# Retention and a quick-GELU layer: transposing q and k by 32x32 squares on VectorE, products of y in order of shape, row decay applied to y

## The chip, the cores and the metric

One core of a Trainium2 chip. The metric is the time of one execution in device microseconds, lower is better. The profile's span is 1.7 us shorter than the time of the execution it was taken from.

## The reference, cut to what matters

```python
batch, n_heads, seq, head_dim = (4, 8, 768, 64)          # q, k, v, float32
n_tokens, d_model, d_ff = (3072, 512, 2048)              # w_in 512x2048, w_out 2048x512, float64

for t in range(S):                                       # retention, per head
    state = gamma * state + outer(k[:, :, t], v[:, :, t])
    y[:, :, t] = scale * (q[:, :, t] @ state)
x = y.transpose(0, 2, 1, 3).reshape(B * S, H * D)        # 3072 x 512
h = x @ w_in
out = (h * (1.0 / (1.0 + np.exp(-1.702 * h)))) @ w_out
```

## The kernel before

Retention runs in 24 chunks of 128 tokens, six for each of the four sequences. A chunk has three stages: `turn` puts channels on partitions, `attend` makes the scores, `finish` makes y and the next state. Four chunks are a block of 512 tokens; a block's layer is 32 units of four 128x512 products, and the chunks of one block run between the units of the block before. The weights come as the bits of float64, in 32 pieces of 512 KB (`raw`), and `narrow` turns one piece into float32 with six VectorE instructions, two of ScalarE and one of GpSimd.

```python
    def load(j):
        b, c = divmod(j, NC)
        for name, src in (("q", q), ("k", k), ("v", v)):
            t = loads.tile([P, H, D], F32, name=name + "_in")
            sp.dma_start(t, src[b, :, c * P:(c + 1) * P, :].rearrange("h p d -> p h d"))
            QKV[name, j] = t
    # ... cut
    def turn(j):
        qn, kn = QKV.pop(("q", j)), QKV.pop(("k", j))
        for x, store in ((qn, QT), (kn, KT)):
            p = ps.tile([P, HP, P], F32, name="pt", tag="att")
            for hp in range(HP):
                pe.transpose(p[:, hp, :], x[:, 2 * hp:2 * hp + 2, :].rearrange("p i d -> p (i d)"), ident)
            t = work.tile([P, HP, P], F32, name="qT" if store is QT else "kT")
            if store is QT:
                dve.tensor_mul(t, p, rowd)
            else:
                act.activation(t, p, AF.Copy)
            store[j] = t
    # ... cut (kd = k times its decay, on GpSimd)
    def finish(j):
        # ... cut
        for hp in range(HP):
            if c:
                pe.matmul(y[:, hp, :], old[:, hp, :], qt[:, hp, :], start=True, stop=False)
            for i in range(2):
                pe.matmul(y[i * D:(i + 1) * D, hp, :], vn[:, 2 * hp + i, :], a[:, i, hp, :],
                          start=not c, stop=True)
        # ... cut
        act.activation(XT[m][:, :, n * P:(n + 1) * P], y, AF.Copy)
    # ... cut
    # chunks of block m between the units of block m - 1 (take runs units, and narrows a weight beside each)
                if j + AHEAD < NCH:
                    load(j + AHEAD)
                turn(j)
                take(per // 4)
                attend(j)
                take(per // 4)
                finish(j)
                take(per - 2 * (per // 4))
                if m == 0:
                    for _ in range(N1 // CB):
                        narrow(pieces.pop(0))      # and fetches the piece three further on, from SyncE's queue
```

Of the kernel before, what the change touches and what calls it, by code (L numbers as in the profile page):

```python
# [8 lines left out]

F32 = mybir.dt.float32  # L10
U32 = mybir.dt.uint32
AF = mybir.ActivationFunctionType
ALU = mybir.AluOpType
P = 128
# [3 lines left out]
    return struct.unpack("<f", struct.pack("<I", bits))[0]  # L18


# Bounds of a float64's high word without its sign, as the float32 of the same bits (which has
# the same order): the exponent below float32's normal numbers, which turns to 0, and 2^128,
# which turns to infinity.
F64_LEAST = _f32((1023 - 127) << 20)
F64_MOST = _f32((1023 + 128) << 20)

# [2 lines left out]
def kernel(  # L29
# [8 lines left out]
    col_decay: bass.AP,  # L38
    out: bass.AP,
):  # L40
    """Retention in chunks of P tokens, its output kept transposed on chip as the x of
    (x @ w_in) * sigmoid(1.702 x @ w_in) @ w_out.

    Within a chunk, y[t] = sum over s <= t of g^(t-s) scale (q[t].k[s]) v[s], plus
    g^(t+1) scale q[t] @ state; then state = g^P state + sum over s of g^(P-1-s) k[s] v[s]^T.
    The weights come as the bits of float64 and are rounded to float32 on chip.
    row_decay[h, t] is scale g^(t+1). col_decay has, by columns: g^-(s+1) [H],
    g^(P-1-s) [H], and g^P [H/2] with its upper half of partitions for a pair's second head.
    """
    nc = tc.nc  # L50
    pe, act, dve, pool, sp = nc.tensor, nc.scalar, nc.vector, nc.gpsimd, nc.sync

    B, H, S, D = q.shape
    NT, DM = out.shape
    DFF = moe_w_in.shape[1]
    HP = H // 2            # pairs of heads: one pair fills the partitions
    NC = S // P            # chunks of a batch
    NCH = B * NC           # chunks
    CB = 4                 # chunks in a block of tokens of the second part
    BT = CB * P  # L60
    NB = NCH // CB
    NFF = DFF // P
# [3 lines left out]
    const = ctx.enter_context(tc.tile_pool(name="const", bufs=1))  # L66
    loads = ctx.enter_context(tc.tile_pool(name="loads", bufs=3))
# [2 lines left out]
    ps_a = ctx.enter_context(tc.tile_pool(name="ps_a", bufs=1, space=bass.MemoryType.PSUM))  # L70
    ps = ctx.enter_context(tc.tile_pool(name="ps", bufs=3, space=bass.MemoryType.PSUM))

# [1 line left out]
    QKV = {}  # L74

    def load(j):
        b, c = divmod(j, NC)
        for name, src in (("q", q), ("k", k), ("v", v)):
            t = loads.tile([P, H, D], F32, name=name + "_in")
            sp.dma_start(t, src[b, :, c * P:(c + 1) * P, :].rearrange("h p d -> p h d"))  # L80
            QKV[name, j] = t

    AHEAD = 2
    rowd = const.tile([P, HP, P], F32, name="rowd")
    cold = const.tile([P, 2 * H + HP], F32, name="cold")
    act.dma_start(cold, col_decay)
# [4 lines left out]
                    ap=[[0, D], [2 * P, HP], [1, P]]),  # L91
        )

    # Weights by pieces of DM columns: w_in's by quarters of its columns, then w_out's by rows.
    W1 = const.tile([P, HP, DFF], F32, name="W1")
    W2 = const.tile([P, NFF, DM], F32, name="W2")
    w1v = moe_w_in.bitcast(U32).rearrange("(c p) (f two) -> p c f two", p=P, two=2)
# [9 lines left out]
            sp.dma_start(RAW[i], PIECES[i][1])  # L107

    def narrow(i):
        """float64 to float32: the high word's 20 bits of fraction with the exponent rebiased, plus  # L110
        the low word at its place, added and so rounded in float32, then the sign."""
        fetch(i + WAHEAD)
        w, x = PIECES[i][0], RAW.pop(i)
        lo, hi = x[:, :, 0], x[:, :, 1]
        m = work.tile([P, DM], F32, name="m")
        e = work.tile([P, DM], F32, name="e")
        r = work.tile([P, DM], F32, name="r")
        mu = m.bitcast(U32)
        dve.tensor_scalar(mu, hi, 0x7FFFFFFF, None, op0=ALU.bitwise_and)  # L119
        dve.tensor_scalar(m, m, F64_MOST, F64_LEAST, op0=ALU.min, op1=ALU.max)  # L120
        # The exponent's bits 10 and 6..0 are those of float32, and 128 more puts bit 10 at bit 7.
        act.activation(m, m, AF.Copy, scale=2.0 ** 16)
        dve.tensor_scalar(mu, mu, 4, 1, op0=ALU.logical_shift_left, op1=ALU.logical_shift_right)  # L123
        dve.tensor_scalar(e.bitcast(U32), mu, 0x7F800000, None, op0=ALU.bitwise_and)  # L124
        act.activation(r, lo, AF.Copy, scale=2.0 ** -52)  # L125
        pool.tensor_mul(r, r, e)  # L126
        dve.tensor_add(m, m, r)  # L127
        dve.scalar_tensor_tensor(w.bitcast(U32), hi, 0x80000000, mu, op0=ALU.bitwise_and, op1=ALU.bitwise_or)  # L128
# [4 lines left out]
        if i < AHEAD - 1:  # L133
            load(i + 1)

# [1 line left out]
    ident = const.tile([P, P], F32, name="ident")  # L137
    make_identity(nc, ident)
    # mask[s, i, hp, t] = g^-(s+1) where s <= t, else 0, for head 2 hp + i
    mask = const.tile([P, 2, HP, P], F32, name="mask")  # L140
    for i in range(2):
        for hp in range(HP):
            h = 2 * hp + i
# [1 line left out]
    m3 = mask.rearrange("s i h t -> s (i h) t")  # L145
    pool.affine_select(out=m3, in_=m3, compare_op=ALU.is_ge, fill=0.0, base=0,
                       pattern=[[0, H], [1, P]], channel_multiplier=-1)
    # two states in turn, block diagonal over a pair's heads
    state = [const.tile([P, HP, P], F32, name=f"state{i}") for i in range(2)]
    for t in state:  # L150
        dve.memset(t, 0.0)

# [1 line left out]
    QT, KT, KD, AT, XT = {}, {}, {}, {}, {}  # L154

    def turn(j):
        """q and k with channels on partitions, q decayed from the chunk's start; k decayed to its end."""
        qn, kn = QKV.pop(("q", j)), QKV.pop(("k", j))
        for x, store in ((qn, QT), (kn, KT)):
            p = ps.tile([P, HP, P], F32, name="pt", tag="att")  # L160
            for hp in range(HP):
                pe.transpose(p[:, hp, :], x[:, 2 * hp:2 * hp + 2, :].rearrange("p i d -> p (i d)"), ident)  # L162
            t = work.tile([P, HP, P], F32, name="qT" if store is QT else "kT")
            if store is QT:
                dve.tensor_mul(t, p, rowd)  # L165
            else:
                act.activation(t, p, AF.Copy)  # L167
            store[j] = t
        if j % NC < NC - 1:
            KD[j] = work.tile([P, H, D], F32, name="kd")  # L170
            pool.tensor_mul(KD[j], kn, cold[:, H:2 * H, None].to_broadcast([P, H, D]))  # L171

    def attend(j):
        p = ps_a.tile([P, 2, HP, P], F32, name="pa")
# [9 lines left out]
    def finish(j):  # L184
        c = j % NC
        old, new = state[c % 2], state[(c + 1) % 2]
        vn, a, qt = QKV.pop(("v", j)), AT.pop(j), QT.pop(j)
        y = ps.tile([P, HP, P], F32, name="py", tag="att")
        for hp in range(HP):
            if c:  # L190
                pe.matmul(y[:, hp, :], old[:, hp, :], qt[:, hp, :], start=True, stop=False)  # L191
            for i in range(2):
                pe.matmul(y[i * D:(i + 1) * D, hp, :], vn[:, 2 * hp + i, :], a[:, i, hp, :],  # L193
                          start=not c, stop=True)
        m, n = divmod(j, CB)
        if n == 0:
            XT[m] = work.tile([P, HP, BT], F32, name="xT")
        act.activation(XT[m][:, :, n * P:(n + 1) * P], y, AF.Copy)  # L198
        if c == NC - 1:
            return  # L200
        kd = KD.pop(j)
        u = ps.tile([P, HP, P], F32, name="pu", tag="att")
        for hp in range(HP):
            h = slice(2 * hp, 2 * hp + 2)
            pe.matmul(u[:, hp, :], kd[:, h, :].rearrange("p i d -> p (i d)"),  # L205
                      vn[:, h, :].rearrange("p i d -> p (i d)"), start=True, stop=True)
        for i in range(2):
            r = slice(i * D, (i + 1) * D)
            if c == 0:
                dve.tensor_copy(new[r, :, r], u[r, :, r])  # L210
            else:
                pool.tensor_mul(new[r, :, r], old[r, :, r],  # L212
                                cold[r, 2 * H:, None].to_broadcast([D, HP, D]))
                dve.tensor_add(new[r, :, r], new[r, :, r], u[r, :, r])  # L214

# [1 line left out]
    GT, PO = {}, {}  # L217

    def up(m, f):
# [22 lines left out]
        return [lambda f=f: up(m, f) for f in range(NFF)] + [  # L242
            lambda n=n, i=i: down(m, n, i) for n in range(CB) for i in range(4)]

# [1 line left out]
    pieces = list(range(len(PIECES)))  # L246
    for m in range(NB + 1):
        todo = units(m - 1) if m else []
# [8 lines left out]
        if m < NB:  # L257
            for n in range(CB):
                j = m * CB + n
# [17 lines left out]


def _decays(n_heads, head_dim):
    """Powers of the heads' decays, which depend on the shapes alone."""  # L280
    import numpy as _np

    gamma = 1.0 - 2.0 ** (-5.0 - _np.arange(n_heads))
    t = _np.arange(P)
    row = gamma[:, None] ** (t + 1) / _np.sqrt(head_dim)
    whole = _np.repeat(gamma.reshape(-1, 2).T ** P, P // 2, axis=0)
    col = _np.concatenate(
        [gamma[None, :] ** -(t[:, None] + 1.0), gamma[None, :] ** (P - 1 - t[:, None]), whole], axis=1)
    return {"row_decay": row.astype(_np.float32), "col_decay": col.astype(_np.float32)}
# [28 lines left out]
```

## Time and profile before

| of the kernel before | us |
|---|---|
| time, median of 2 executions | 856.79 (856.55 to 857.04) |
| first 128x512 product (block 0 starts) | 65.15 |
| first product of block 1 | 209.82 |
| from there to the end | 645.3 |
| TensorE busy | 821.2 of the span's 855.1 |

The table cuts the span at two landmarks: the **head** (loads, weights and chunks 0 to 3, then block 0 with chunks 4 to 7) and the **steady part** after it, where TensorE doesn't stop.

What feeds the head is SyncE's queue, which issues all loads of q, k, v and the weights. In time order, some of its lines (start, length, engine, line, the transfer, how many in a row):

```profile
0.81 0.43 SPq L80 DMA_DIRECT2D q_in<-in_q_dram  x1
...
1.92 0.86 SPq L80 DMA_DIRECT2D v_in<-in_v_dram  x1
2.82 0.97 SPq L107 DMA_DIRECT2D raw<-in_moe_w_in_dram  x1
...
31.79 3.77 SPq L80 DMA_DIRECT2D v_in<-in_v_dram  x1
...
130.72 11.32 SPq L107 DMA_DIRECT2D raw<-in_moe_w_out_dram  x4
```

A chunk costs this queue three issues. Load 3 is the one that block 0 still needs, and what the head waits for is the narrowing.

### The profile page before, as it was taken

The numbers are of one execution on the slowest core, as the hardware profiler recorded it, in microseconds if no ns is written. First come the engines' busy times: TensorE is split into PE (matmuls) and PEld (weight loads), VectorE is DVE, ScalarE is ACT, GpSimd is POOL, SyncE is SP. The second block draws the span as 40 slices with busy tenths as digits, with TensorE's granted clock in tenths as the row PEclk, the third lists the DMA queues.
The fourth block names the chain that finished last, engine by engine and source line by source line (L and its number), as shares of the span: only waits on it lengthen the run. The fifth ranks groups of instructions, "written<-read, shape, count | busy, mean of one in ns | idle before, by whom it ended". The sixth has DMA issues, their size and how long they took to land.

```text
span 855.1 us, 7038 instructions
## 1 busy us (share of the span) xinstructions
PE 821.2 (96%) x2816; PEld 408.3 (48%) x2816; DVE 239.1 (28%) x434; ACT 126.4 (15%) x210; POOL 84.6 (10%) x91
## 2 busy tenths in 40 slices
PE   4679979999999999999999999999999999999998
PEld 3545434445545544544545454445445445444443
DVE  4877888311222110222111222111122111012000
ACT  2234444000111000111000111100011100011000
POOL 3433333201101000101011000011010000000000
PEclk9759989999999999999999999999999999999999
DMA  9476454012010210110110110111100000000000
GB/s 224 133 183 162 149 164 144 25 38 61 13 25 13 50 38 25 50 25 13 38 49 25 37 36 14 25 46 41 38 13 0 1 12 25 12 1 0 13 13 25
DMA packets 83663, 42.66 MB, mean 50 GB/s; under 512 B 75952, under 2 KB 76464, under 8 KB 83632
## 3 DMA queue, kind: packets, MB, share of 16 engines
q1 hardware_dynamic: 79488, 35.66, 16.5%
q10 hardware_dynamic: 4144, 6.57, 2.1%
q8 instruction: 22, 0.36, 0.2%
q14 instruction: 9, 0.07, 0.0%
HBM read 35.92 MB, written 6.29 MB: 49 GB/s over the span
## 4 chain that ended last, share of the span: by engine, by line
PE 87%; DVE 7%; POOL 3%; issue 2%; DMA 1%; ACT 0%; SPq 0%; POOLq 0%; ACTq 0%; DVEq 0%
PE po L234 39%; PE ph L222 34%; PE py L193 4%; PE py L191 3%; PE pa L178 3%; POOL r L126 2%; PE pu L205 2%; PE pt L162 2%; DVE m L127 2%; DVE e L124 1%; DVE m L123 1%; DMA raw<-in_moe_w_in_dram 1%; DVE W L128 1%; DVE m L119 1%; DVE m L120 1%
## 5 line engine op out<-in xcount | busy, mean ns | idle before, releaser
L222 PE MATMUL ph<-xT,W 128*128 128x512 f32 x768 | 340.8, 601 | 0.0
L234 PE MATMUL po<-W,gT 128*128 128x512 f32 x768 | 336.0, 594 | 0.0
L222 PEld LDWEIGHTS ph<-xT,W 128*128 128x128 f32 x768 | 145.5, 193 | 174.0 <-issue 170.9
L234 PEld LDWEIGHTS po<-W,gT 128*128 128x128 f32 x768 | 143.5, 190 | 170.9 <-issue 169.7
L226 DVE TENSOR_TENSOR gT<-ph,sg 128x512 f32<-128x512 f32 x96 | 66.2, 690 | 209.5 <-ACT sg L224 209.5
L224 ACT ACTIVATE sg<-ph 128x512 f32<-128x512 f32 x96 | 57.2, 595 | 261.8 <-PE ph L222 261.7
L237 DVE COPY o<-po 128x512 f32<-128x512 f32 x24 | 16.6, 692 | 239.2 <-PE po L234 239.2
L171 POOL TENSOR_TENSOR kd<-k_in,cold 128x512 f32<-128x512 f32 x20 | 21.1, 1054 | 451.8 <-PE pu L205 258.1
L193 PE MATMUL py<-at,v_in 128*64 128x128 f32 x384 | 46.8, 321 | 14.4 <-DVE at L181 14.4
L181 DVE TENSOR_TENSOR at<-pa,mask 128x512 f32<-128x512 f32 x48 | 31.2, 683 | 67.1 <-PE pa L178 67.1
L126 POOL TENSOR_TENSOR r<-r,e 128x512 f32<-128x512 f32 x32 | 42.3, 1322 | 72.6 <-DVE e L124 72.4
L198 ACT ACTIVATE xT<-py 128x512 f32<-128x512 f32 x24 | 14.3, 596 | 189.3 <-PE py L193 189.3
L191 PE MATMUL py<-qT,state 128*128 128x128 f32 x160 | 41.3, 344 | 0.0
L178 PE MATMUL pa<-qT,kT 64*128 64x128 f32 x384 | 30.4, 302 | 8.6 <-DVE qT L165 7.8
L191 PEld LDWEIGHTS py<-qT,state 128*128 128x128 f32 x160 | 28.0, 209 | 20.5 <-issue 19.7
L178 PEld LDWEIGHTS pa<-qT,kT 64*128 64x128 f32 x384 | 25.6, 203 | 24.9 <-issue 14.6
L193 PEld LDWEIGHTS py<-at,v_in 128*64 128x64 f32 x384 | 22.5, 148 | 29.6 <-DVE at L181 17.4
L167 ACT ACTIVATE kT<-pt 128x512 f32<-128x512 f32 x24 | 14.3, 596 | 142.4 <-PE pt L162 142.4
L127 DVE TENSOR_TENSOR m<-m,r 128x512 f32<-128x512 f32 x32 | 26.2, 819 | 19.4 <-POOL r L126 19.4
L125 ACT ACTIVATE r<-raw 128x512 f32<-128x512 uint32 x32 | 21.8, 681 | 53.9 <-DVE m L127 43.8
L205 PE MATMUL pu<-v_in,kd 128*128 128x128 f32 x160 | 25.8, 307 | 0.0
L212 POOL TENSOR_TENSOR state<-state,cold 64x256 f32<-64x256 f32 x32 | 20.1, 629 | 49.9 <-DVE state L214 31.8
(25 smaller groups left out, 218.0 us busy)
## 6 DMA issues: line engine op xcount, KB each, us to landing
raw<-in_moe_w_in_dram SPq DMA_DIRECT2D x16, 512.0 KB, 4.5
raw<-in_moe_w_out_dram SPq DMA_DIRECT2D x16, 512.0 KB, 3.3
q_in<-in_q_dram SPq DMA_DIRECT2D x24, 256.0 KB, 4.0
k_in<-in_k_dram SPq DMA_DIRECT2D x24, 256.0 KB, 4.4
v_in<-in_v_dram SPq DMA_DIRECT2D x24, 256.0 KB, 3.3
out_dram<-o ACTq DMA_DIRECT2D x24, 256.0 KB, 2.0
rowd<-in_row_decay_dram ACTq DMA_DIRECT2D x2, 128.0 KB, 5.5
cold<-in_col_decay_dram ACTq DMA_DIRECT2D x1, 10.0 KB, 2.8
```

Of the source, the lines that this page charges most:

```text
L125: act.activation(r, lo, AF.Copy, scale=2.0 ** -52)
L126: pool.tensor_mul(r, r, e)
L127: dve.tensor_add(m, m, r)
L178: pe.matmul(p[:, i, hp, :], KT[j][r, hp, :], QT[j][r, hp, :], start=True, stop=True)
L181: dve.tensor_mul(AT[j][:, i], p[:, i], mask[:, i])
L191: pe.matmul(y[:, hp, :], old[:, hp, :], qt[:, hp, :], start=True, stop=False)
L193: pe.matmul(y[i * D:(i + 1) * D, hp, :], vn[:, 2 * hp + i, :], a[:, i, hp, :], start=not c, stop=True)
L205: pe.matmul(u[:, hp, :], kd[:, h, :].rearrange("p i d -> p (i d)"), vn[:, h, :].rearrange("p i d -> p (i d)"), start=True, stop=True)
L222: pe.matmul(p, W1[:, c, f * P:(f + 1) * P], XT[m][:, c, :], start=(c == 0), stop=(c == HP - 1))
L224: act.activation(s, p, AF.Sigmoid, scale=1.702)
L226: dve.tensor_mul(g, p, s)
L234: pe.matmul(p, GT[m, f][:, n * P:(n + 1) * P], W2[:, f, :], start=(f == 0), stop=(f == NFF - 1))
```

## The change

The intent: take the eight transposes of a chunk off TensorE, which sets the time, and spare it changes of shape. The VectorE instruction used, `dve.transpose`, turns each 32x32 block where it stands; so the DMA puts each 32x32 square of q and k at the place of its mirror image, and one such instruction then finishes the transpose of 128x512. As q is no longer decayed on its way out of PSUM, the decay moves to y. k is also loaded in rows (`kn`), for the state.

```diff
     def load(j):
-        for name, src in (("q", q), ("k", k), ("v", v)):
+        for name, src in (("q", q), ("k", k)):
+            t = loads.tile([P, HP, Q4, C4], F32, name=name + "_sq")        # Q4 = 4, C4 = 32
+            for i in range(2):
+                for d in range(D // C4):
+                    r0 = i * D + d * C4
+                    for hp in range(HP):
+                        sp.dma_start(
+                            t[r0:r0 + C4, hp],
+                            src[b, 2 * hp + i, c * P:(c + 1) * P, d * C4:(d + 1) * C4].rearrange(
+                                "(s p) d -> p s d", p=C4))
+            QKV[name, j] = t
+        for name, src in (("kn", k), ("v", v)):
+            if name == "kn" and c == NC - 1:
+                continue
             t = loads.tile([P, H, D], F32, name=name + "_in")
             sp.dma_start(t, src[b, :, c * P:(c + 1) * P, :].rearrange("h p d -> p h d"))
 ... (turn: the PE transposes, the decay of q and the copy of k go)
-            p = ps.tile([P, HP, P], F32, name="pt", tag="att")
-            for hp in range(HP):
-                pe.transpose(p[:, hp, :], x[:, 2 * hp:2 * hp + 2, :].rearrange("p i d -> p (i d)"), ident)
+            dve.transpose(t.rearrange("p h t -> p (h t)"), QKV.pop((name, j)).rearrange("p h s d -> p (h s d)"))
 ... (finish)
+        if c:
+            for hp in range(HP):
+                pe.matmul(y[:, hp, :], old[:, hp, :], qt[:, hp, :], start=(hp == 0), stop=False,
+                          skip_group_check=True)
         for hp in range(HP):
-            if c:
-                pe.matmul(y[:, hp, :], old[:, hp, :], qt[:, hp, :], start=True, stop=False)
             for i in range(2):
                 pe.matmul(y[i * D:(i + 1) * D, hp, :], vn[:, 2 * hp + i, :], a[:, i, hp, :],
-                          start=not c, stop=True)
+                          start=(not c and hp == 0), stop=(hp == HP - 1), skip_group_check=True)
-        act.activation(XT[m][:, :, n * P:(n + 1) * P], y, AF.Copy)
+        dve.tensor_mul(XT[m][:, :, n * P:(n + 1) * P], y, rowd)
```

More of the change, by code (lines that the diff above doesn't have):

```diff
@@ L6 @@
 from concourse import mybir
-from concourse.masks import make_identity
 from concourse._compat import with_exitstack
@@ L74 @@
     QKV = {}
+    Q4, C4 = P // 32, 32
     def load(j):
         b, c = divmod(j, NC)
-        for name, src in (("q", q), ("k", k), ("v", v)):
+        for name, src in (("q", q), ("k", k)):
[12 more added lines that the diff above has]
+                continue
             t = loads.tile([P, H, D], F32, name=name + "_in")
@@ L134 @@
             load(i + 1)
-    ident = const.tile([P, P], F32, name="ident")
-    make_identity(nc, ident)
     mask = const.tile([P, 2, HP, P], F32, name="mask")
@@ L156, in turn @@
     def turn(j):
-        qn, kn = QKV.pop(("q", j)), QKV.pop(("k", j))
-        for x, store in ((qn, QT), (kn, KT)):
-            p = ps.tile([P, HP, P], F32, name="pt", tag="att")
-            for hp in range(HP):
-                pe.transpose(p[:, hp, :], x[:, 2 * hp:2 * hp + 2, :].rearrange("p i d -> p (i d)"), ident)
+        for name, store in (("q", QT), ("k", KT)):
             t = work.tile([P, HP, P], F32, name="qT" if store is QT else "kT")
-            if store is QT:
-                dve.tensor_mul(t, p, rowd)
-            else:
-                act.activation(t, p, AF.Copy)
+            dve.transpose(t.rearrange("p h t -> p (h t)"), QKV.pop((name, j)).rearrange("p h s d -> p (h s d)"))
             store[j] = t
@@ L170, in turn @@
             KD[j] = work.tile([P, H, D], F32, name="kd")
-            pool.tensor_mul(KD[j], kn, cold[:, H:2 * H, None].to_broadcast([P, H, D]))
+            pool.tensor_mul(KD[j], QKV.pop(("kn", j)), cold[:, H:2 * H, None].to_broadcast([P, H, D]))
     def attend(j):
```

## The prediction

> **What bounds the kernel now.** I read the page's strip of 40 slices first, then the chain that ended last, then the time order of TensorE over one period, and last the stretches.
>
> ```profile
> PE   4679979999999999999999999999999999999998
> DVE  4877888311222110222111222111122111012000
> PE 87%; DVE 7%; POOL 3%; issue 2%; DMA 1%; ACT 0%; SPq 0%; POOLq 0%; ACTq 0%; DVEq 0%
> ```
>
> There are two regimes. From the seventh slice (about 145 us) on, TensorE is 90% busy or more in every slice and VectorE mostly at 10 to 20%; before that VectorE is at 70 to 80% (it turns the float64 weights into float32) and TensorE has gaps. The chain says the same: 87% of the span is TensorE. The windows put numbers on it:
>
> ```profile
> 65.15:143.53 78.38, 72.31 (x226) 34.44 (x225) 67.14 (x137) 35.21 (x59) 26.79 (x22) 0.92 0.53 155
> 143.53:209.10 65.57, 65.57 (x235) 32.43 (x234) 16.85 (x33) 5.29 (x9) 9.33 (x10) 1.00 0.15 41
> 209.10:741.40 532.30, 532.30 (x1882) 262.96 (x1880) 96.23 (x154) 57.31 (x96) 23.25 (x31) 1.00 0.11 28
> 0.00:65.15 65.15, 41.13 (x224) 30.22 (x225) 44.36 (x91) 19.00 (x30) 25.18 (x30) 0.78 0.73 181
> ```
>
> The columns are stretch, length, busy time of PE, weight loads, VectorE, ScalarE and GpSimd, clock, DMA share, GB/s. From 143.53 us TensorE has no idle time at full clock, so what leaves its queue there leaves the time. Before 65.15 us (chunks 0 to 3, first weights) it is idle a third of the time, and from 65.15 to 143.53 a little. The last 114 us hold no chunk and don't change.
>
> One period, chunk 15, in time order (start, length, engine, line):
>
> ```profile
> 441.85 0.60 PE L162 MATMUL pt<-ident,q_in 128*128 128x128 f32 x4
> 442.29 0.60 PE L162 MATMUL pt<-ident,k_in 128*128 128x128 f32 x4
> 442.73 7.03 PE L234 MATMUL po<-W,gT 128*128 128x512 f32 x16
> ...
> 457.75 0.38 PE L191 MATMUL py<-qT,state 128*128 128x128 f32 x2
> 458.07 0.44 PE L193 MATMUL py<-at,v_in 128*64 128x128 f32 x4
> 458.44 0.49 PE L191 MATMUL py<-qT,state 128*128 128x128 f32 x2
> 458.85 0.44 PE L193 MATMUL py<-at,v_in 128*64 128x128 f32 x4
> ...
> 460.80 1.16 PE L205 MATMUL pu<-v_in,kd 128*128 128x128 f32 x8
> 461.79 13.90 PE L234 MATMUL po<-W,gT 128*128 128x512 f32 x32
> ```
>
> Go by the starts, as the ends are modelled. The eight transposes take 442.73 - 441.85 = 0.88 us. The products of y take 460.80 - 457.75 = 3.05 us, and alternate eight times between shapes 128*128 and 128*64. The next chunk's transposes start at 475.53, so a period is 33.68 us.
>
> **What the Trainium skill says.** (1) "TensorEngine Tiling (Array Packing)", Tiling Modes, Key Properties: changing the tiling mode, not just the tile, drains TensorE. The trace agrees: in chunks that begin a sequence there are no state products, and the period is 31.75 us (342.76 to 374.50), 1.93 us shorter, although the eight missing products (recorded as two instructions each) of 128 columns are worth only 8 x 0.107 = 0.86 us (0.429 us per 512 columns, from 13.7 us for 32, gives 0.107 per 128). The other 1.07 us is six changes of shape, 0.18 us each. (2) "VectorE: DVE Perf Modes", The three transpose paths: VectorE transposes only within 32x32 blocks, 311 ns for 128x128 bf16. Nothing in this trace transposes on VectorE; I estimate 0.69 us for 128x512 float32, the measured mean of this trace's tensor-tensor operations of that size. (3) "DMA: Bandwidth & Descriptors", Rules for kernel authors: coalesce many small transfers; under 64 KB one pays mostly overhead. The new loads are 16 KB. (4) Same page, Issuing engines are not separate DMA queues: the sequencer's time to initiate a DMA "is usually small relative to the DMA itself". Here that turns round: the trace has issues of 0.34 to 0.39 us when nothing holds them, while 16 KB at the 224 GB/s seen in the first slice is 0.07 us.
>
> **The change part by part.**
>
> *Removed from TensorE:* 8 transposes in each of 24 chunks, 0.88 us each. *Regrouped:* four state products, then the eight 128*64 products: two changes of shape in place of eight, 1.07 us less in each of the 20 chunks with a state. So a period becomes 33.68 - 1.95 = 31.73 us. Where TensorE is the bound (chunks 8 to 23, from 209.1 us on): 14 x 1.95 + 2 x 0.88 = **29 us saved**.
>
> *VectorE:* per chunk two transposes (2 x 0.69) and the decay of y (0.69) in place of the decay of q (0.69): +1.4 us of a 32 us period in which it works about 6. ScalarE loses two copies of 0.60 us. Both are hidden in the steady part. In the head, eight chunks x 1.4 = 11 us of VectorE are added to some 111 us of work in 143 us; it stays below full.
>
> *DMA:* q and k of one chunk become 32 loads of 16 KB (128-byte runs), and k is loaded once more in rows (not for the last chunk of a sequence). With v that is 34 issues per chunk in place of 3, all from SyncE's queue, which also fetches the raw weights:
>
> ```profile
> 60.99 0.34 SPq L107 DMA_DIRECT2D raw<-in_moe_w_in_dram  x1
> 61.42 0.39 SPq L80 DMA_DIRECT2D v_in<-in_v_dram  x1
> ```
>
> From one start to the next is 0.43 us; with gaps of 0.05 to 0.10 after issues of 0.34 I take 0.42 us: 34 x 0.42 = **14.3 us per chunk**. In a period of 32 us that is hidden. In the head it isn't: the order of the built program has the queue as load 0, raw 0, load 1, raw 1 and 2, load 2, raw 3 to 6, load 3, raw 7 to 10, and so on. Four raws take about 4 x 512 KB at 310 GB/s = 6.6 us of the DMA engines; each load waits on the completion of the eighth before it (eight completion counters in turn, by the built order), so after four raws the queue loses about 3 us. So I get, as times of issue: load 0 ends at 15 us, load 1 at 30, load 2 at 45, raws 3 to 6 at 47, load 3 at 65, load 4 at 85, load 5 at 104, load 6 at 124; the last weights near 160 to 180.
>
> *Head, summed:* load 3 lands about 67; two transposes, the scores, the mask, y and its decay take some 8 us: the first block's products start at **75 us** in place of 65. From there TensorE is the bound again: 32 units x 3.43 = 110 us, and chunks 4 to 7 need 22.0 us beside them now (periods of 33.68, 32.78, 31.75 and 33.68 us less 8 x 3.43 each), less 3 x 1.95 + 0.88 = 15.3 us then: 125 us. Before, this block took 209.1 - 65.2 = 144 us for 132 us of work, so 12 us of waits and cold clock; I keep 12. It ends at 75 + 125 + 12 = 212 us in place of 209: **3 us lost**. The savings of chunks 4 to 7 are inside this figure.
>
> *Sum:* 855.1 + 3 - 29 = 829 us of span; the measured time is 1.7 us above the span now: **830 us** rounded, 3% faster.
>
> **The rivals.**
>
> (a) *Issue becomes the bound of the head.* For it: 34 issues per chunk, one queue, weights behind them. Against: 0.42 us each leaves a chunk in some 19 us, and TensorE needs 31 us for a chunk with its eight units. If an issue costs 0.6 us with its wait (eight in flight, 4.8 us to land instead of the 2.0 us of the stores), load 3 moves by 4 x 34 x 0.18 = 24 us and the last weights by more: about 855 us, the same as before.
>
> (b) *DMA engines become the bound.* A chunk now has 4096 runs of 128 bytes and 2048 of 256. In 442 to 448 us, q and k (2048 runs) took about 38 us of engine time: 18.6 ns a run. If 128 bytes cost as much, a chunk is 114 us over 16 engines, 7 us: less than the issue. Only four raws and a load together (14 us) come near the head's 19 us.
>
> (c) *The head hides everything, as it was bound by VectorE.* If an issue takes 0.3 us, load 3 ends near 47 us, the old 65 us holds, and chunks 4 to 7 give up to 7 us: about 815 to 820 us.
>
> (d) *The steady part doesn't collect its 29 us,* because ScalarE's sigmoids or the stores wait on loads. Against: TensorE runs 600 us without a gap, VectorE has 80% free there, and loads are two chunks ahead or more. A store that shares a counter with a load could wait, but the built order leaves it about 10 us. Then 840 to 855.
>
> **Range and chances.** The 29 us come from measured durations, and I trust them to 4 us. The head is open by -12 (rival c) to +24 us (rival a). So 812 to 853 with the middle at 830. 2% faster is below 839.7 us: the head may lose 13 us in place of 3, an issue of 0.5 us. I give that 0.75, within 2% 0.22, slower 0.03.
>
> **What would show it right or wrong.** Transposes gone from TensorE; y as eight then sixteen recorded products in some 1.95 us; a period of 31.7 us; VectorE transposes near 0.69 us; SyncE issues 0.40 to 0.45 us apart in the head, with the first 128x512 product near 75 us and the second block's start near 212. It is wrong if the issues lie 0.5 us or more apart, if transposes on VectorE stand in front of weight narrowing and hold it, or if TensorE shows idle time after 215 us.

## The result, and the profile after

The changed kernel takes **866.93 us** (median of 2, 866.69 to 867.17) against 856.79: ratio 1.0114, 95% interval 1.0084 to 1.0143. So it is 1% slower, within 2%, where 830 us (3% faster) was predicted, and outside the range of 812 to 853. A ratio here is the mean time of one kernel's fast runs over that of the other's of the same rounds, so not quite the ratio of the medians.

| us | before | after | predicted for after |
|---|---|---|---|
| block 0 starts | 65.15 | 91.46 | 75 |
| block 1 starts | 209.82 | 247.53 | 212 |
| from there to the end | 645.3 | 617.5 | 617 (829 - 212) |
| span | 855.1 | 865.0 | 829 |

The whole miss is in the head, 35.5 us of it; the steady part came out as predicted to half a microsecond. The strip of 40 slices of the kernel after, and its chain of waits:

```profile
PE   1532899886899999999999999999999999999998
...
DVE  2447867786523311122320232221132210111100
...
DMA  4454444444333232322212211210000000000000
...
PE 79%; SPq 6%; DVE 6%; DMA 5%; POOL 2%; issue 2%; ACT 0%; ACTq 0%; POOLq 0%; DVEq 0%
```

TensorE is at 9 tenths in every slice only from the twelfth on. In the first three slices VectorE works at 2 to 4 tenths where it was at 4 to 8, so it isn't what the head waits for there, and the DMA engines are at 4 to 5 tenths. The chain has a new member: 6% is SyncE's queue, which was 0%.

The stretches (busy time of PE, weight loads, VectorE, ScalarE, GpSimd; clock, DMA share, GB/s), cut at the landmarks:

```profile
0.00:91.46 91.46, 29.79 (x184) 24.59 (x184) 42.67 (x83) 12.09 (x18) 19.94 (x23) 0.70 0.47 113
91.46:247.53 156.07, 135.28 (x432) 62.89 (x433) 105.95 (x196) 40.11 (x64) 42.36 (x34) 0.96 0.42 111
247.53:751.42 503.89, 503.89 (x1754) 247.57 (x1753) 115.32 (x183) 38.21 (x64) 24.38 (x32) 1.00 0.18 38
```

To 91.46 us VectorE works 42.67 us, less than half; before it was 44.36 of 65.15. From 247.53 TensorE is busy all the time: no rival in which the steady part doesn't pay is left. One period of it in time order:

```profile
443.28 1.16 PE L184 MATMUL pa<-qT,kT 64*128 64x128 f32 x16
...
451.34 1.05 PE L197 MATMUL py<-qT,state 128*128 128x128 f32 x8
452.33 1.09 PE L201 MATMUL py<-at,v_in 128*64 128x128 f32 x16
453.35 1.16 PE L213 MATMUL pu<-v_in,kd 128*128 128x128 f32 x8
...
475.04 1.16 PE L184 MATMUL pa<-qT,kT 64*128 64x128 f32 x16
```

The transposes are gone, y's products take 453.35 - 451.34 = 2.01 us in place of 3.05, and the period is 475.04 - 443.28 = 31.76 us (predicted 31.73). Now SyncE's queue in the head:

```profile
0.81 7.81 SPq L86 DMA_DIRECT2D q_sq<-in_q_dram  x16
8.66 7.54 SPq L86 DMA_DIRECT2D k_sq<-in_k_dram  x16
16.25 0.43 SPq L95 DMA_DIRECT2D kn_in<-in_k_dram  x1
16.72 0.58 SPq L95 DMA_DIRECT2D v_in<-in_v_dram  x1
17.35 0.98 SPq L122 DMA_DIRECT2D raw<-in_moe_w_in_dram  x1
...
56.66 2.49 SPq L122 DMA_DIRECT2D raw<-in_moe_w_in_dram  x4
59.20 13.38 SPq L86 DMA_DIRECT2D q_sq<-in_q_dram  x16
72.63 7.54 SPq L86 DMA_DIRECT2D k_sq<-in_k_dram  x16
...
81.39 2.41 SPq L122 DMA_DIRECT2D raw<-in_moe_w_in_dram  x4
...
214.05 0.35 SPq L122 DMA_DIRECT2D raw<-in_moe_w_out_dram  x1
```

A chunk's squares go out at 0.47 to 0.49 us each with nothing in their way (7.54 and 7.81 us for 16). Behind four raws, q's 16 take 13.38 us. Load 3 is out at 81.3 us, 10 us before block 0 starts; it was 30 us ahead before. The last weight is issued at 214.05 us; before, the last four went out between 130.72 and 142. The queue's own waits (in total, times, longest) name two things that hold it: its squares wait for completions of raws, and a raw waits for VectorE to narrow an earlier one and so free its buffer. All nine waits of the second kind lie in block 0, after 130 us. The groups by shape say who waits for the squares (busy, mean ns, idle ahead of them and its releasers):

```profile
SPq L122 <- DVE W L143: 35.8, 9, 11.0
SPq L86 <- DMA raw<-in_moe_w_in_dram: 18.9, 15, 1.7
```

```profile
L173 DVE STREAM_TRANSPOSE kT<-k_sq 128x512 f32<-128x512 f32 x24 | 16.8, 699 | 16.3 <-DMA k_sq<-in_k_dram 16.3
```

VectorE stood 16.3 us before these for want of k's squares. And the transfer of a square is short (16 KB land 1.8 us after their issue, by the list of DMA issues), while the row of issues is long.

### The profile page after: what moved, and what is told of

It is laid out like the page before. It is cut to its first block, busy times and chain, and to the rows that moved or that the text cites. A ratio compares the mean times of both kernels' runs of the same rounds, so it can differ in the third digit from the quotient of the medians.

```text
span 865.0 us, 7451 instructions
## 1 busy us (share of the span) xinstructions
PE 778.8 (90%) x2624; PEld 383.3 (44%) x2624; DVE 278.5 (32%) x482; ACT 100.0 (12%) x162; POOL 86.7 (10%) x89
## 4 chain that ended last, share of the span: by engine, by line
PE 79%; SPq 6%; DVE 6%; DMA 5%; POOL 2%; issue 2%; ACT 0%; ACTq 0%; POOLq 0%; DVEq 0%
PE po L242 35%; PE ph L230 35%; SPq L86 6%; DMA raw<-in_moe_w_in_dram 3%; PE py L201 3%; PE pa L184 3%; PE pu L213 2%; POOL r L141 2%; PE py L197 2%; DVE m L142 1%; DVE e L139 1%; DVE m L138 1%; DVE W L143 1%; DVE m L135 1%; DMA raw<-in_moe_w_out_dram 1%
## 5 line engine op out<-in xcount | busy, mean ns | idle before, releaser
L242 PE MATMUL po<-W,gT 128*128 128x512 f32 x768 | 342.8, 603 | 19.1 <-DVE W L143 19.1
L230 PE MATMUL ph<-xT,W 128*128 128x512 f32 x768 | 335.6, 594 | 0.9 <-DVE xT L206 0.8
L242 PEld LDWEIGHTS po<-W,gT 128*128 128x128 f32 x768 | 145.5, 193 | 201.4 <-issue 172.0
L177 POOL TENSOR_TENSOR kd<-kn_in,cold 128x512 f32<-128x512 f32 x20 | 21.2, 1062 | 397.5 <-issue 176.9
L197 PE MATMUL py<-qT,state 128*128 128x128 f32 x160 | 24.2, 300 | 32.8 <-DVE qT L173 32.8
L184 PEld LDWEIGHTS pa<-qT,kT 64*128 64x128 f32 x384 | 26.6, 210 | 41.0 <-issue 21.8
L197 PEld LDWEIGHTS py<-qT,state 128*128 128x128 f32 x160 | 23.1, 212 | 42.1 <-DVE qT L173 24.9
L201 PE MATMUL py<-at,v_in 128*64 128x128 f32 x384 | 31.7, 293 | 4.4 <-DVE at L187 4.4
L137 ACT ACTIVATE m<-m 128x512 f32<-128x512 f32 x32 | 19.9, 627 | 36.0 <-DVE m L135 35.8
L213 PEld LDWEIGHTS pu<-v_in,kd 128*128 128x128 f32 x160 | 21.8, 209 | 4.5 <-issue 3.8
```

The costliest lines, as they stand in the source:

```text
L184: pe.matmul(p[:, i, hp, :], KT[j][r, hp, :], QT[j][r, hp, :], start=True, stop=True)
L197: pe.matmul(y[:, hp, :], old[:, hp, :], qt[:, hp, :], start=(hp == 0), stop=False, skip_group_check=True)
L213: pe.matmul(u[:, hp, :], kd[:, h, :].rearrange("p i d -> p (i d)"), vn[:, h, :].rearrange("p i d -> p (i d)"), start=True, stop=True)
L230: pe.matmul(p, W1[:, c, f * P:(f + 1) * P], XT[m][:, c, :], start=(c == 0), stop=(c == HP - 1))
L242: pe.matmul(p, GT[m, f][:, n * P:(n + 1) * P], W2[:, f, :], start=(f == 0), stop=(f == NFF - 1))
```

## The experiments

The theory: the **number of issues on SyncE's queue** sets the head, through load 3 first and through the weights, which stand in the same queue, after that. The rivals: the 128-byte runs load the DMA engines; the transposes that VectorE got hold up the narrowing; the regrouped y or the decay on VectorE made a new wait. All kernels but one are correct. They ran in two batches, each with the kernel before on the same chip: its median was 856.66 in the first (the first four below) and 856.45 in the second (the other four). Of the single executions, e_fewissues, e_kact and e_rawpool have the steady part of the changed kernel, which all three share (617.4, 617.4 and 617.5 us against 617.5).

### The regrouping of y alone (e_yorder)

```diff
 on the kernel before
-        for hp in range(HP):
-            if c:
-                pe.matmul(y[:, hp, :], old[:, hp, :], qt[:, hp, :], start=True, stop=False)
+        if c:
+            for hp in range(HP):
+                pe.matmul(y[:, hp, :], old[:, hp, :], qt[:, hp, :], start=(hp == 0), stop=False, ...)
+        for hp in range(HP):     # then the eight 128*64 products, as in the change
```

> The kernel before, with the regrouping of y's products alone (loads and transposes as before). The head stays bound by the weights and VectorE, so the gain is 1.07 us in each of the 14 to 20 chunks with a state where TensorE is the bound: every theory expects 836 to 842 us, a period of 32.6 us in chunks 13 to 16.

836.95 us, ratio 0.9778 (0.9759 to 0.9798): 2% faster by this part alone. The steady part is 630.75 us in place of 645.3: 14.55 us for 14 chunks with a state, 1.04 us each, which is 0.17 us for each of six changes of shape if the gain is all theirs (the edit also changes the start and stop flags of the products; that wasn't tested apart). The reordering is innocent, and worth half of the steady gain.

### Few issues, the same short runs (e_fewissues; wrong result)

q and k are still cut in runs of 128 bytes, but each in two loads of 128 KB in place of sixteen of 16 KB. The squares land in wrong places, so the result is wrong; every instruction that works on them is the same.

```diff
-            for i in range(2):
-                for d in range(D // C4):
-                    r0 = i * D + d * C4
-                    for hp in range(HP):
-                        sp.dma_start(t[r0:r0 + C4, hp], ...)
+            for d in range(D // C4):
+                sp.dma_start(
+                    t.rearrange("p h s c -> p (h s) c")[:, d * H:(d + 1) * H, :],
+                    src[b, :, c * P:(c + 1) * P, d * C4:(d + 1) * C4].rearrange("h p d -> p h d"))
```

> The changed kernel with the same 4096 runs of 128 bytes of q and k per chunk, but in 4 loads in place of 32 (they land in wrong places, so the result is wrong on purpose). Theory 'issue' (SyncE's queue issues 34 loads of 0.47 us per chunk, with the weights behind them): the head's loss goes, second block starts near 209 us, 826 to 832 us in all. Rival 'runs' (128-byte runs and more bytes fill the DMA engines): 860 to 867, as they are unchanged. Rival 'VectorE' (1.4 us more per chunk and transposes in front of the weights in its queue): only part goes, 838 to 845.

830.06 us (one execution), where the issue theory stood. In the time order of its TensorE:

```profile
62.51 11.35 PE L226 MATMUL ph<-xT,W 128*128 128x512 f32 x20 [1.78 <-DVE xT L202]
...
210.90 7.03 PE L226 MATMUL ph<-xT,W 128*128 128x512 f32 x16
```

With the same bytes in the same runs, and the same work on VectorE, block 0 starts at 62.51 and block 1 at 210.90 us; the rest is 617.4 us. Both rivals fall: short runs cost nothing that shows, and VectorE's added work costs 210.90 - 204.25 = 6.6 us of head (204.25 is where block 1 starts in e_yorder, which has none of it), net of what TensorE saves there by its transposes. 36.6 of the 37.7 us by which the change moved block 1 go away with the issues alone, and 247.53 - 210.90 = 36.6 us is also close to the whole miss of the prediction.

### k's squares from ScalarE's queue (e_kact)

```diff
-                        sp.dma_start(
+                        (sp if name == "q" else act).dma_start(
```

> The changed kernel with k's 16 squares of a chunk issued from ScalarE's queue, q's from SyncE's. Theory 'issue': SyncE has 18 issues per chunk, so the first block's products start near 65 to 75 us in place of 91; ScalarE's activations of the weights now stand behind its own issues, so not all of it comes: 835 to 850. Rival 'runs': 862 to 868. If the eight completion counters that all loads share in turn are the limit and not the issue: 862 to 868 too.

850.52 us (one execution, correct): just outside what was expected, in time (835 to 850) and in the start of block 0, which is 79.03 us (65 to 75). Splitting the row of issues over two queues brings load 3 forward, but block 1 starts only at 231.37: 152.3 us for block 0 in place of 156.1. ScalarE's instructions stand behind its own issues now, and it has two in every weight; that this is what block 0 still pays is my reading, not tested apart. For chunks 0 to 6, q's 16 squares took 9.2 to 11.0 us in SyncE's queue, where 16 squares take 7.5 with nothing in their way; so their spacing isn't the price of an issue alone. The queue's waits say what is added: to 130 us SyncE waited for k's squares, which ScalarE had issued, 16.7 us ahead of q's squares and 21.8 us ahead of raws. In the built program the loads of both queues share eight completion counters in turn, so the two queues weren't free of each other. Half the issues on a second queue gave back 16 us of 37: it helps, and is not as good as not issuing.

### The weights from GpSimd's queue (e_rawpool)

```diff
-            sp.dma_start(RAW[i], PIECES[i][1])
+            pool.dma_start(RAW[i], PIECES[i][1])
```

> The changed kernel with the weights fetched from GpSimd's queue, q, k and v from SyncE's. Theory 'issue': the weights no longer stand behind squares and squares no longer behind weights; load 3 ends at about 4 x 34 x 0.47 = 64 us, the first block starts at 72 to 78 us and isn't held by the second weights: 836 to 848. Rival 'runs': 860 to 868. Rival 'VectorE': 850 to 862, for the narrowing is still behind the transposes.

868.88 us (one execution, correct): a miss, by 20 us at least. By this run's own forecast the number is the one of the rival "runs" (860 to 868); e_fewissues excludes that rival, so the cause must lie elsewhere. Three stretches of its profile, then one line of its VectorE in time order:

```profile
40.00:80.00 40.00, 10.77 (x56) 9.02 (x56) 34.01 (x64) 11.33 (x18) 19.84 (x21) 0.52 0.63 149
80.00:117.84 37.84, 15.49 (x89) 12.69 (x89) 33.70 (x57) 9.79 (x15) 20.29 (x22) 0.50 0.70 183
117.84:249.66 131.82, 129.48 (x432) 62.61 (x433) 68.08 (x119) 23.13 (x38) 28.40 (x29) 0.98 0.37 82
```

```profile
106.40 0.71 DVE L173 STREAM_TRANSPOSE kT<-k_sq 128x512 f32<-128x512 f32 x1
```

Taking the weights out of the queue didn't bring load 3 forward: it still ends at 83 us by the time order of SyncE's queue, since a row of 16 squares takes 7.5 to 12.5 us here: to 118 us the queue waited 12.4 us for earlier squares to land (weights move beside them now; that this is why wasn't tested). And it shifted work: with weights coming early, VectorE narrows ahead and is nearly full from 40 to 117.84 us (34.01 of 40 us, 33.70 of 37.84). k's squares of chunk 3 were there at 83 us and were transposed at 106.40, behind that narrowing. Block 0 started 26 us later, at 117.84, and was 24 us shorter (131.82 us, with 129.48 of TensorE), because its weights were done. The sum is the same: here late weights were only exchanged for a later block 0, as the transpose stood behind that narrowing in VectorE's order and the squares were no earlier.

### The old path for chunks 0 to 7, squares from chunk 8 on (e_headold)

```diff
 on the changed kernel
+    HEAD = 8
     def load(j):
+        if j < HEAD:      # q, kn and v in three loads of 256 KB, as before
+            ...
+            return
     def turn(j):
+            if j < HEAD:  # four PE transposes into PSUM and a ScalarE copy; the decay stays on y
+                ...
+                continue
```

> A mend of the changed kernel: chunks 0 to 7 load q, k and v in 3 loads and TensorE transposes q and k (ScalarE copies both), chunks 8 to 23 load squares. Theory 'issue in the head': the second block starts at 209 us less some 7 us of regrouping (the kernel before with the regrouping alone ran 20 us faster), and the later chunks keep their 28.5 us: 818 to 828 us. If the loss lay elsewhere (decay of y on VectorE, regrouped products), it stays near 850 to 867.

**824.54 us** (823.59 to 826.01), ratio 0.9625 (0.9605 to 0.9646), correct: faster than both kernels by 4% and 5%. Block 0 starts at 56.51 us, block 1 at 206.05, and the rest takes 617.35 us. Its strip:

```profile
PE   5669898799999999999999999999999999999998
...
DVE  4888888511323201313212223212223111122100
```

VectorE is back at 8 tenths from the second slice on. The steady part keeps all of its gain while the head loses nothing: 247.53 - 206.05 = 41.5 us of head is what the squares of the first eight chunks had cost against the old path.

### Squares over two chunks in one load (e_pairs)

```diff
+            if c % 2:
+                continue
-            t = loads.tile([P, HP, Q4, C4], F32, name=name + "_sq")
+            t = loads.tile([P, HP, 2 * Q4, C4], F32, name=name + "_sq", bufs=2)
-                            src[b, 2 * hp + i, c * P:(c + 1) * P, ...
+                            src[b, 2 * hp + i, c * P:(c + 2) * P, ...
-            QKV[name, j] = t
+            QKV[name, j], QKV[name, j + 1] = t[:, :, :Q4], t[:, :, Q4:]
```

(To make room, kT and kd have one buffer in place of two.)

> The changed kernel with each square load reaching over two chunks: 32 issues of 32 KB per pair of chunks in place of 64 of 16 KB, as many runs of 128 bytes (k's turned copy and its decayed copy have one buffer each to make room). Theory 'issue': up to chunk 3 there are 64 fewer issues of 0.47 to 0.49 us, so the first block starts 25 to 30 us earlier (62 to 68 us), 828 to 842 us in all. Rival 'runs': 860 to 868.

840.16 us (839.15 to 840.84), ratio 0.9803 (0.9781 to 0.9825), correct; the interval contains 2%, so against that mark the verdict is unclear: it is faster, and by about 2%. With half the issues of squares, block 0 starts at 63.97 us: the first-block cost is gone. Block 1 starts at 222.00: block 0 still lasts 158 us. This isn't a clean test of weights behind squares, though: the kernel also lost buffers, and in block 0 its queue waits 67.1 us, in 17 times, for VectorE to narrow a weight (35.8 in nine in the changed kernel).

### Twice the issues (e_double)

```diff
+                        for s in range(2):
-                            t[r0:r0 + C4, hp],
-                            src[b, 2 * hp + i, c * P:(c + 1) * P, ...
+                                t[r0:r0 + C4, hp, 2 * s:2 * s + 2],
+                                src[b, 2 * hp + i, c * P + s * 64:c * P + (s + 1) * 64, ...
```

> The changed kernel with every square load cut in two (64 loads of 8 KB per chunk, the same runs and bytes). Theory 'issue': 32 x 0.47 = 15 us more per chunk; the first block starts some 60 us later (about 150), and in the steady part 66 issues of 0.47 us are 31 us, about the period of 31.76, so the queue binds or nearly: 960 to 1010 us. Rival 'runs': below 875.

1003.35 us (one execution, correct). The first row of squares in SyncE's queue:

```profile
0.80 15.21 SPq L87 DMA_DIRECT2D q_sq<-in_q_dram  x32
```

15.21 us for 32 issues is 0.48 us again, at half the size: it is a price for the issue, not for its bytes (behind raws the 32 take up to 20 us). Here the steady part pays too, 1001.6 - 354.3 = 647.3 us in place of 617.5 (block 1 starts at 354.30): 66 issues of 0.47 us are 31 us, and a period is 31.76. This completes a row of doses, by the issues that SyncE's queue makes up to the end of load 3 (seven weights included; weights in the same queue, squares in this queue or few loads):

| kernel | issues | block 0 starts, us |
|---|---|---|
| e_double | 271 | 149.1 |
| after | 143 | 91.5 |
| e_pairs | 79 | 64.0 |
| e_fewissues | 31 | 62.5 |
| before, e_yorder, e_headold | 19 | 65.2, 60.1, 56.5 |

From 79 to 143 the start moves by 27.5 us (0.43 us per issue), from 143 to 271 by 57.6 us (0.45 each): nearly the whole price of an issue reaches the end. Below some 80 issues the line is flat, near 60 us: something else sets the start there. For the kernel before, VectorE at 7 and 8 tenths points to the narrowing; that wasn't tested.

### The change without the regrouping (e_noy)

```diff
 on the changed kernel: y's products in the order of the kernel before
-        if c:
-            for hp in range(HP):
-                pe.matmul(y[:, hp, :], old[:, hp, :], qt[:, hp, :], start=(hp == 0), ...)
         for hp in range(HP):
+            if c:
+                pe.matmul(y[:, hp, :], old[:, hp, :], qt[:, hp, :], start=True, stop=False)
```

> The changed kernel with the products of y in their old order. Every theory: 1.07 us more in each chunk with a state from the second block on (13 or 14 chunks), a little in the first block where waits hide part: 880 to 886 us.

881.40 us (one execution, correct). Block 0 starts at 93.16 and block 1 at 247.73, as in the changed kernel; the steady part is 632.0 us. So the transposes are worth 645.3 - 632.0 = 13.3 us, the regrouping 14.55, together 27.85, and the change's steady part is 645.3 - 617.5 = 27.8 us shorter: the parts add up. The transposing part alone loses 25.0 us against the kernel before of the same batch (881.40 to 856.45).

## Why the prediction was wrong

**What held.** The eight transposes at 0.88 us, the 1.04 us of y, the period of 31.76 us, the 0.70 us of a VectorE transpose (0.69 said), and the steady saving: 27.8 us against 29. TensorE doesn't idle after block 1 starts; no store and no ScalarE wait came in. Rival (d) was rightly set aside.

**What failed is the head**, "3 us lost" where 37.7 us were lost. Three of its steps:

1. "34 x 0.42 = 14.3 us per chunk". The 0.42 us was read from issues of 256 and 512 KB; the squares' are 0.47 to 0.49 us apart, so load 0 ended at 17.3 us rather than 15, and with the stalls behind the first raws load 2 was out at 56.6 us rather than 45. That the price doesn't depend on the size is shown by e_double.
2. "after four raws the queue loses about 3 us". It lost nearly 6 (13.38 us in place of 7.54 for q's squares). Both terms together made load 3 end at 81.3 us rather than 65 (143 issues of 0.475 us are 68 us; the squares' waits for raws to 92 us are 12.8, in ten); its own cycle was 24.7 us for 38 issues (56.66 to 81.39), 0.65 us each; block 0 started at 91.5 in place of 75. That is 16.5 us of the miss.
3. "I keep 12" for the waits and cold clock of block 0, beside 125 us of work. Block 0 lasted 156.1 us, not 137: 31 in place of 12. TensorE stood idle for 156.07 - 135.28 = 20.8 us of it (6.1 before), 19.1 of them for weights not narrowed yet:

```profile
L242 PE MATMUL po<-W,gT 128*128 128x512 f32 x768 | 342.8, 603 | 19.1 <-DVE W L143 19.1
```

The weights were late: the last was issued at 214 us and not "near 160 to 180". To 153 us this is the row of issues: every four raws stand behind the squares of a chunk, and start 23 to 25 us apart (81.39, 106.72, 130.58, 153.15). After that the queue also waits for VectorE, 10.7 us ahead of the raw at 173.17 and 11.0 ahead of the last, with squares standing behind those raws; VectorE in turn had the masks of chunks 6 and 7 in front of that narrowing and stood 2.8 and 5.1 us for their scores. So each held the other, and how much of the lateness is the row and how much this ring of waits was not separated. The working knew when the last weights would come, and didn't carry it into the sum.

16.5 + 19 is the 35.5 us. This splits the miss by landmark and not by cause, for a block 0 that starts early has longer to wait for its weights: with few issues it starts at 62.5 and still lasts 148.4 us, and in e_rawpool it starts at 117.84 and lasts 131.8. By cause the record has one figure, e_fewissues: the issues are 36.6 us of block 1's start. Rival (a), that issues become the bound, was the right one; that its 0.6 us per issue comes near the 0.65 seen, and its 855 us within 12, is partly luck. It let each square land after 4.8 us; they land after 1.8, and the 0.65 is 0.47 for an issue with waits for raws on top. The argument against it (19 us per chunk, TensorE needs 31) compared the queue with the wrong stage: in chunks 0 to 3 there are no units to hide behind. Rival (b), the DMA engines, fell: their share of the first stretch went from 0.73 down to 0.47. (Its 310 GB/s names no source; the prediction's own stretch gives 155 / 0.53 = 292 GB/s at full share.) Rival (c) fell too: an issue took 0.47 us and not 0.3, and the old 65 us didn't hold.

**What stays open.** The trace shows SyncE's squares waiting on completions of raws, 18.9 us in 15 waits for those of w_in and 3.6 us in 3 for those of w_out; how much of that is the rotation of eight completion counters (the program gives them to its loads in turn, and each load waits for the eighth before it), and how much the raws' own speed beside the squares, was not separated. And VectorE's head grew by 20 us (129.0 to 148.6 of busy time to block 1): 16 more instructions of 0.7 us explain 11 us, while two forms of the narrowing took 0.58 and 0.55 us a piece in place of 0.42 and 0.45 (0.52 and 0.42 in e_fewissues, with the same instructions). The cause of that was not tested; with the issues gone all of VectorE's part is 6.6 us net.

## What to carry to other kernels

Count DMA issues by queue and by stage, and multiply by a measured spacing: a load cut into 32 is free where work covers it (34 issues, 16 us, in a period of 31.76; at 66 it no longer was) and sets the time where nothing does, as at a kernel's start. If a queue also carries something that everything waits for (here the weights), sum its issues up to that thing before asking about bandwidth. And where a change is good in one stage and bad in another, use it in the good one only: e_headold took the 27.8 us and left the head as it was.

## What the Trainium skill lacked or had wrong

- "DMA: Bandwidth & Descriptors", Issuing engines are not separate DMA queues: that initiating is "usually small relative to the DMA itself" comes with no duration there. The runs show 0.47 to 0.49 us for each issue, the same for 16 KB (7.54 us for 16) and for 8 KB (15.21 us for 32), and 0.43 to 0.45 us per issue arriving at the start of block 0. Elsewhere the page has about 50 ns of sequencer dispatch (Anatomy of one DMA, the GpSimd path), a tenth of it, and, in a passage on trn3, 512 sequencer cycles per `DmaMemcpy` for "previous generations", without a time and without naming trn2.
- "TensorEngine Tiling (Array Packing)", Key Properties: the drain at a change of tiling mode has no cost there. Here one between 128*128 and 128*64 took 0.17 us, if all that the regrouping gained is theirs (14.55 us over 14 chunks of six).
